# A seventh zero fill that leaves out one transfer engine

## The chip, the cores and the metric

The kernel runs on one core of a Trainium2 chip. The core has five engines that run their own instruction streams: TensorE (PE: matrix products, transposes), VectorE (DVE), ScalarE (ACT), GpSimd (POOL) and SyncE (SP). Data moves between the chip's main memory (HBM) and the on-chip memory through 16 transfer (DMA) engines. A transfer is issued by an engine's instruction stream; here nearly all are issued by POOL and some by SP. A transfer of 128 rows is cut into 16 shares of 8 rows, one for each transfer engine; each engine works through its shares in order, and raises the transfer's semaphore when its share is done.

The metric is the device time of one execution in microseconds (us). Before the change it is 599.19 us, the median of three runs (598.75 to 599.40).

## What is computed

The reference is a forward and a backward pass of one decoding step: one token of width 1024 through an adaptive layer norm with attention over the last 4096 positions of a key/value cache, and then through a gated feed-forward block. Cut to what matters:

```python
x = A_x
mod = (silu(c) @ w_mod).reshape(1, 6, 1, -1)
sa, ca, ga, sb, cb, gb = mod[:, 0], mod[:, 1], ..., mod[:, 5]
h = layernorm(x) * (1 + ca) + sa
x = x + ga * attention(h, k_cache[:, :, -4096:], v_cache[:, :, -4096:], wq, wo)
h = layernorm(x) * (1 + cb) + sb
x = x + gb * ((sigmoid(h @ w_gate) * (h @ w_up)) @ w_down)
out, grads = x, vjp(grad_out)   # gradients of x, caches, wq, wo, w_gate, w_up, w_down, c, w_mod
```

All tensors are bfloat16. The caches are [1, 4, 65536, 128]. Only the last 4096 positions of each head are used, so the gradients of both caches are zero in the first 61440 positions of each of the four heads: 2 x 4 x 61440 x 128 values, 120 MiB of zeros to be written.

## The kernel before

Everything that is loaded or computed lives in one large on-chip tile (`arena`) and some small ones. The weights are read once; their gradients, outer products of a column and a broadcast row, are made in place by VectorE and ScalarE, and stored. In order of time the kernel does the following. It loads w_mod, the key cache, wq and the value cache, and computes the query, the scores and the softmax. From about 70 us to 155 us it forms a product of keys and values (`n_ps`, L640), then from about 155 to 310 us a long product with w_o (`b_ps`, L695). The feed-forward block's loads, products, outer products and stores run in seven rounds (L1023 to L1068) until about 477 us. The last stage stores the gradients of w_o (`dwo`, L1142, in rows of 8 KB), of w_mod (`sec`, L1136, and `s2`, L1190), of wq (`dwq_tile`, L1186) and of the caches' last 4096 positions (`grad_kv`, L1167). The last ten stores go through SyncE's queue (`tail`, L1307 to L1314), the others through POOL's.

The order of the instructions is written out by hand. The zeros are written by 120 fills of 1 MiB each, and the calls `zero(n)` put them between the other transfers of POOL's queue, as many at each place as tables such as `Z_N`, `Z_B`, `Z_FFN` and `Z_END` say. A fill takes one of 120 regions, 128 rows of 8 KB, from the list `zleft`, and writes it from a small tile of zeros. `zero_rest`, called once after the query's products (L479), is issued at 54.5 us.

A fill is either wide or narrow. The list `NARROW` gives the places in the order of issue, counted from 0, at which a fill is narrow. A wide fill writes all 128 rows, 8 rows on each of the 16 transfer engines. A narrow fill is made of three instructions: POOL's cursor for the choice of transfer engines is reset (L160), a small transfer of `NS` = `SKIP` + 1 = 5 rows is issued (L162), which is meant for the engines 0 to 4, and then rows 8 to 127 of the region are written as 60 rows of two pieces (L165), which are meant for the 15 engines from 5 on, around to 3. By the code's plan engine 4 has no share of the narrow fill, and the others have the same share as in a wide one. The first 8 rows of the narrow regions, 64 KB each, are left over. They form `rest`, a block of 8 rows. Most of it is written by `zero_rest` with one transfer over 16 rows of pieces (L362) and a small one (L365); the pieces that are still missing are the small transfers of L162.

`keep`, `nlen` and `ncount` follow from the length of `NARROW`. The last stage's fills stand at these places:

```python
Z_END = (1, 2, 1, 0, 0)
zero(Z_END[0])          # L1194, before the stores of dwo(0) to dwo(3)
zero(Z_END[1])          # L1218, after dwo(5): two fills
zero(Z_END[2])          # L1244, after dwo(7): the last fill
```

Of the kernel before, what the change touches and what calls it, by code (L numbers as in the profile page):

```python
# [34 lines left out]
SCALE = DH ** -0.5  # L35
KIB = 512
SKIP = 4
NARROW = (15, 45, 75, 95, 104, 113)


def spread(total, n):
# [17 lines left out]
def kernel(  # L59
# [70 lines left out]

    narrow = zregions[0:len(NARROW)]
    wide = zregions[len(NARROW):]
    zleft = []
    while narrow or wide:
        if narrow and (len(zleft) in NARROW or not wide):
            zleft.append((narrow.pop(0), True))
        else:
            zleft.append((wide.pop(0), False))
    nlen = len(NARROW)
    ncount = list(range(1, nlen + 1))  # L140
# [1206 lines left out]
```

## Time and profile before

| what | value |
|---|---|
| median of three runs | 599.19 us (598.75 to 599.40) |
| the profiled execution: its time, its span | 599.24 us, 597.5 us |
| busy: PE, DVE, ACT, POOL | 68%, 56%, 44%, 26% of the span |
| moved by the transfer engines | 246.63 MB, 413 GB/s in the mean |
| HBM read, written | 60.30 MB, 185.60 MB |
| POOL's queue (q0), SP's queue (q1): share of 16 engines | 95.1%, 13.0% |
| wide fills | 114, 1024 KB each, 15.4 us from issue to landing |
| narrow fills | 6, 960 KB each, 12.8 us |
| the small transfers of narrow fills | 6, 2.5 KB each, 11.2 us |
| `zero_rest` | 360 KB, 10.7 us, and 9 KB, 10.4 us |
| the chain that ended last | PE 44%, DMA 22%, DVE 20% |

The span runs from the first to the last instruction of the profiled execution; the execution's own time is 1.7 us longer. Busy time of an engine says how much it worked, not what the kernel waited for. The page's slices cut the span into 40 equal parts, and their digits are tenths of a part. The shares of the two queues add up to more than 100%, since packets of both queues are under way on an engine at once. The page's chain of work follows the last instruction back to what released it, step by step. A transfer's time to landing runs from its issue to the moment at which all 16 transfer engines have done their share; most of it is the wait behind the transfers that were issued earlier.

### The profile page before, as it was taken

The numbers are of one execution on the slowest core, as the hardware profiler recorded it, in microseconds if no ns is written. First come the engines' busy times: TensorE is split into PE (matmuls) and PEld (weight loads), VectorE is DVE, ScalarE is ACT, GpSimd is POOL, SyncE is SP. The second block draws the span as 40 slices with busy tenths as digits, with TensorE's granted clock in tenths as the row PEclk, the third lists the DMA queues.
The fourth block names the chain that finished last, engine by engine and source line by source line (L and its number), as shares of the span: only waits on it lengthen the run. The fifth ranks groups of instructions, "written<-read, shape, count | busy, mean of one in ns | idle before, by whom it ended". The sixth has DMA issues, their size and how long they took to land.

```text
span 597.5 us, 11109 instructions
## 1 busy us (share of the span) xinstructions
PE 407.2 (68%) x4618; PEld 275.0 (46%) x4644; DVE 335.4 (56%) x642; ACT 264.9 (44%) x409; POOL 155.9 (26%) x254
## 2 busy tenths in 40 slices
PE   3997688999999989999983437245345285685210
PEld 3995334334344545546653326245334264485110
DVE  3654499999511010070018585678787886878350
ACT  2489514567211014212135275465664834893110
POOL 3113123222222213222221242323424252132100
PEclk9999699999999999999995565665555586955555
DMA  8999999999999999999999999999999999999996
GB/s 349 417 418 423 411 427 409 429 422 426 428 417 425 423 427 424 422 423 423 424 396 414 419 411 416 410 369 416 408 406 412 419 420 424 423 422 426 425 424 286
DMA packets 44003, 246.63 MB, mean 413 GB/s; under 512 B 5086, under 2 KB 5086, under 8 KB 22497
## 3 DMA queue, kind: packets, MB, share of 16 engines
q0 software_dynamic: 36656, 218.64, 95.1%
q1 hardware_dynamic: 7248, 27.27, 13.0%
q8 instruction: 36, 0.59, 0.4%
q14 instruction: 15, 0.11, 0.0%
q10 hardware_dynamic: 48, 0.01, 0.0%
HBM read 60.30 MB, written 185.60 MB: 412 GB/s over the span
## 4 chain that ended last, share of the span: by engine, by line
PE 44%; DMA 22%; DVE 20%; issue 5%; ACT 5%; POOL 0%; DVEq 0%; ACTq 0%; POOLq 0%; SPq 0%
PE b_ps L695 18%; DMA out_dram<-arena 14%; DVE arena L210 7%; PE n_ps L640 6%; DVE arena L206 5%; DMA arena<-in_B_w_down_dram 4%; DVE arena L193 4%; DMA arena<-in_B_w_gate_dram 3%; PE t_ps L602 2%; PE fold_ps L879 2%; PE tp_wq L457 2%; PE w_ps L398 2%; PE tp_side L840 1%; PE tp_k L438 1%; ACT arena L459 1%
## 5 line engine op out<-in xcount | busy, mean ns | idle before, releaser
L695 PE MATMUL b_ps<-arena 128*128 128x512 bf16 x493 | 113.4, 379 | 1.1 <-issue 0.2
L169 POOL DMA_DIRECT2D out_dram<-zeros x114 | 62.4, 549 | 175.1 <-DMA out_dram<-zeros 46.1
L193 DVE TENSOR_TENSOR arena<-arena 128x2048 bf16<-128x2048 bf16 x64 | 76.5, 1223 | 2.3 <-PE n_ps L640 0.3
L695 PEld LDWEIGHTS <-arena 128*128 128x128 bf16 x512 | 48.8, 98 | 55.8 <-issue 2.9
L210 DVE CUSTOM_DVE_ANT_0 arena<-arena,scr 128x1024 bf16<-128x1024 bf16 x56 | 66.3, 1221 | 9.7 <-ACT scr L995 9.7
L640 PE MATMUL n_ps<-arena 128*128 128x512 bf16 x249 | 65.1, 378 | 6.9 <-DVE arena L193 5.0
L841 ACT COPY arena<-tp_side 128x1024 bf16<-128x1024 bf16 x54 | 52.9, 1015 | 37.4 <-PE tp_side L840 37.4
L957 PE MATMUL fg<-h_bf,arena 128*128 128x1 bf16 x448 | 16.1, 166 | 52.0 <-DMA arena<-in_B_w_up_dram 31.4
L840 PE MATMUL tp_side<-ident_bf,arena 128*128 128x128 bf16 x432 | 47.9, 292 | 3.9 <-ACT arena L841 2.1
L840 PEld LDWEIGHTS <-arena 128*128 128x128 bf16 x432 | 41.5, 137 | 6.4 <-issue 6.1
L640 PEld LDWEIGHTS <-arena 128*128 128x128 bf16 x256 | 24.6, 97 | 41.6 <-issue 16.2
L241 ACT ACTIVATE arena<-scr,h 128x1024 bf16<-128x1024 bf16 x35 | 38.5, 1142 | 2.7 <-DVE dh2acc L210 2.3
L957 PEld LDWEIGHTS <-arena 128*128 128x128 bf16 x448 | 14.1, 105 | 55.0 <-DMA arena<-in_B_w_up_dram 33.1
L202 DVE CAST arena<-b_ps 128x512 bf16<-128x512 f32 x6 | 4.2, 692 | 61.6 <-PE b_ps L695 61.6
L210 DVE CUSTOM_DVE_ANT_0 arena<-arena,b1k 128x1024 bf16<-128x1024 bf16 x24 | 28.4, 1220 | 18.1 <-PE fg L975 18.1
L1176 ACT ACTIVATE arena<-ps_kv 128x512 bf16<-128x512 f32 x48 | 26.1, 681 | 27.2 <-PE ps_kv L1172 27.0
L1172 PE MATMUL ps_kv<-junk,arena 8*128 8x128 bf16 x256 | 26.6, 300 | 14.5 <-DVE arena L206 12.7
L872 POOL DMA_DIRECT2D out_dram<-arena x28 | 22.2, 798 | 50.9 <-ACT arena L241 36.2
L604 ACT CAST arena<-t_ps 128x512 bf16<-128x512 f32 x56 | 30.1, 589 | 12.1 <-PE t_ps L602 12.1
L1172 PEld LDWEIGHTS <-arena 8*128 8x128 bf16 x256 | 24.7, 138 | 16.2 <-issue 16.2
L459 ACT COPY arena<-tp_wq 128x1024 bf16<-128x1024 bf16 x23 | 21.7, 1042 | 8.2 <-PE tp_wq L457 8.2
L206 DVE TENSOR_SCALAR arena<-arena,cs_col 128x4096 bf16<-128x4096 bf16 (+1 forms) x16 | 16.2, 1031 | 10.4 <-DMA out_dram<-arena 10.3
(308 smaller groups left out, 637.8 us busy)
## 6 DMA issues: line engine op xcount, KB each, us to landing
out_dram<-zeros POOLq DMA_DIRECT2D x114, 1024.0 KB, 15.4
out_dram<-arena POOLq DMA_DIRECT2D x28, 1024.0 KB, 18.7
out_dram<-arena POOLq DMA_DIRECT2D x30, 512.0 KB, 12.0
out_dram<-arena SPq DMA_DIRECT2D x20, 512.0 KB, 9.3
arena<-in_A_wq_dram POOLq DMA_DIRECT2D x8, 1024.0 KB, 20.3
arena<-in_A_wo_dram POOLq DMA_DIRECT2D x8, 1024.0 KB, 11.9
arena<-in_w_mod_dram POOLq DMA_DIRECT2D x7, 1024.0 KB, 18.0
arena<-in_B_w_down_dram SPq DMA_DIRECT2D x14, 512.0 KB, 9.0
```

Source lines behind the costliest of these rows:

```text
L169: ins = nc.gpsimd.dma_start(out=region.bitcast(FP32), in_=zeros[:, :])
L193: return nc.vector.tensor_tensor(out=out, in0=a, in1=b, op=op)
L206: return nc.vector.tensor_scalar(out=out, in0=a, scalar1=s1, scalar2=None, op0=op0)
L210: return nc.vector.tensor_tensor_reduce(out=out, in0=w, in1=b, scale=1.0, scalar=0.0, op0=ALU.mult, op1=ALU.add, accum_out=acc)
L241: return nc.scalar.activation(out=out, in_=b, func=ACT.Copy, scale=col)
L604: nc.scalar.copy(out=o, in_=ps)
L640: mm = nc.tensor.matmul(nbank[k][:, :], lhsT=k_nat[:, g, t_ * DH:(t_ + 1) * DH], rhs=vp[:, t_ % 2, 4 * k:4 * k + 4, :].rearrange("p h d -> ...
L695: mm = nc.tensor.matmul(bbank[p][k][:, :], lhsT=a4[:, p, h, :], rhs=wo_t[u][:, a, k * 512:(k + 1) * 512], start=(i == 0 and a == 0), stop= ...
L840: nc.tensor.transpose(tp[:, i * P:(i + 1) * P], blk[:, i * P:(i + 1) * P], ident_bf[:, :])
L841: nc.scalar.copy(out=blk if dst is None else dst, in_=tp[:, :])
L957: nc.tensor.matmul(gu[:, col:col + 1], lhsT=ug_v[:, q % 2, j // 4, j % 4, k, f0:f0 + 255:2], rhs=h2_bf[:, j:j + 1], start=(j == 0 and i == ...
L1172: nc.tensor.matmul(ps[:, t4 * DH:(t4 + 1) * DH], lhsT=rows[32 * g:32 * g + HG, t_ * P:(t_ + 1) * P], rhs=hd[32 * g:32 * g + HG, :], start= ...
```

## The change

One number is added to `NARROW`:

```diff
-NARROW = (15, 45, 75, 95, 104, 113)
+NARROW = (15, 45, 75, 95, 104, 113, 117)
```

The fill at place 117 of 0 to 119 becomes narrow: the third from last, which is the first of the two fills at L1218. At that place POOL now issues the cursor's reset, the small transfer of 5 rows and the narrow fill of 120 rows, in place of a wide fill. `nlen` goes from 6 to 7, so `rest` grows from 6 x 64 KB to 7 x 64 KB, and the transfers of `zero_rest` grow with it: the pieces of L362 from 720 to 840 elements of 4 bytes, those of L365 from 768 to 896. Region 6 of the list becomes narrow too, and the wide fills take the regions after it, so that each writes the region that the next one wrote before. The number of 1-MiB places, their places in POOL's queue, and all instructions of the other engines stay as they are.

## The prediction

> **What bounds the kernel now.** I read the page's slices of the transfer engines first, then the transfers at the very end, then the chain that ended last, then the issues around the changed fill.
>
> ```profile
> DMA  8999999999999999999999999999999999999996
> GB/s 349 417 418 423 411 427 409 429 422 426 428 417 425 423 427 424 422 423 423 424 396 414 419 411 416 410 369 416 408 406 412 419 420 424 423 422 426 425 424 286
> ```
>
> The 16 transfer engines are busy in every slice, mostly at 410 to 427 GB/s; only the last slice falls far, to 6 tenths and 286 GB/s. So the kernel is as long as its transfers, and what is left to win lies where not all 16 work. The end in finer windows (DMA share is the last column but one):
>
> ```profile
> 585.00:590.00 5.00, 0.00 (x0) 0.00 (x0) 0.00 (x0) 0.00 (x0) 0.00 (x0) 0.50 1.01 421
> 590.00:591.00 1.00, 0.00 (x0) 0.00 (x0) 0.00 (x0) 0.00 (x0) 0.00 (x0) 0.50 0.99 406
> 591.00:592.00 1.00, 0.00 (x0) 0.00 (x0) 0.00 (x0) 0.00 (x0) 0.00 (x0) 0.50 0.84 344
> 592.00:593.00 1.00, 0.00 (x0) 0.00 (x0) 0.00 (x0) 0.00 (x0) 0.00 (x0) 0.50 0.53 217
> 593.00:594.00 1.00, 0.00 (x0) 0.00 (x0) 0.00 (x0) 0.00 (x0) 0.00 (x0) 0.50 0.21 86
> 594.00:595.00 1.00, 0.00 (x0) 0.00 (x0) 0.00 (x0) 0.00 (x0) 0.00 (x0) 0.50 0.06 25
> 595.00:596.00 1.00, 0.00 (x0) 0.00 (x0) 0.00 (x0) 0.00 (x0) 0.00 (x0) 0.50 0.07 29
> ```
>
> A share of 0.06 is one engine of 16, at 25 to 29 GB/s. From 594 to 596 us one engine works alone. The trace's completion records say it exactly: every transfer over all engines raises its semaphore 16 times, once for each engine. For the last store (issued at 576.94) the 16 arrivals are, in us:
>
> ```
> 591.31 591.39 592.08 592.13 592.68 592.73 592.83 592.90
> 592.90 592.96 592.97 593.73 594.04 594.19 594.24 596.54
> ```
>
> One engine is 2.30 us behind the next. The chain and SyncE say that nothing but transfers is left there:
>
> ```profile
> 543.94 21.55 DMA out_dram<-arena
> ...
> 565.51 5.05 DVE arena L206 x8
> ...
> 571.78 4.31 DVE arena L206 x6
> ```
>
> ```profile
> 574.79 0.72 SPq L1188 DMA_DIRECT2D out_dram<-arena  x1
> 575.60 2.53 SPq L1192 DMA_DIRECT2D out_dram<-arena  x2
> ```
>
> VectorE's last work ends at 576.1 us and the last store is issued at 576.94, some 19.6 us before it has landed. The end is the backlog of the latest engine and no engine's arithmetic.
>
> **Is the late engine the one that a narrow fill leaves out?** The trace does not number the engines, but the arrivals identify it. Around the narrow fill issued at 178 us, the arrivals relative to their median run: one of them creeps, +0.40, +0.47, +0.59, +0.62 over four transfers; after the narrow fill that one is gone, a new earliest one stands at -1.76, and it creeps again, -1.61, -1.49, while the other 15 keep their places. The one left out thus moved by 0.62 + 1.76 = 2.38 us. Around the narrow fill at 98 us one moves from +0.41 to -1.91, 2.32 us, and then creeps by about 0.1 us per fill (-1.91, -1.79, -1.70, -1.60). So the engine left out is the one that loses about 0.1 us in each fill. Before the last narrow fill (issued at 478) the latest arrival creeps the same way, +1.03, +1.25, +1.38, +1.53; after it nothing is later than +0.81. From 513 us on the latest arrival creeps once more: +0.94, +1.09, then with two steps back to +1.53, +1.93, +2.12, and up to +3.42 at 556. Creep and place agree: the late engine of the end is the one left out. That is a reading of order and drift, not a numbered record, and a rival below doubts it.
>
> **The change part by part.**
>
> *The seventh narrow fill.* It replaces the first of the two wide fills at L1218, issued at 493.81. A narrow fill leaves 64 KB of its region out, the share of one engine; the two moves above price it at 2.32 and 2.38 us for that engine; I take 2.35. For the other 15 the pair (small transfer plus narrow fill) took 2.47, 2.44, 2.23 and 2.39 us on the median arrival at the four narrow fills with no SyncE traffic beside them, against 2.44 for a wide fill: between -0.21 and +0.03; I take 0.
>
> *More small remainder.* The rest transfers at L362 and L365 grow by 7/6. L362 moved the median arrival from 63.51 to 64.45, 0.94 us, on all engines; a sixth more is 0.16 us for each of them. Ends: 0 (it lands early, and time between could absorb it, though no slice shows room) and 0.3 (double, as its rows get another odd length). I take 0.16.
>
> *POOL's issue.* One more instruction (0.61 us) and a longer one (0.67 for 0.53) at 493.8, with a cursor reset that takes no visible time:
>
> ```profile
> 477.92 0.61 POOL L162 DMA_DIRECT2D out_dram<-zeros  x1
> 478.51 0.67 POOL L165 DMA_DIRECT2D out_dram<-zeros  x1
> 479.17 0.59 POOL L169 DMA_DIRECT2D out_dram<-zeros  x1
> ...
> 493.28 0.53 POOL L1145 DMA_DIRECT2D out_dram<-arena  x1 [0.97 <-DVE arena L206]
> 493.81 0.54 POOL L169 DMA_DIRECT2D out_dram<-zeros  x1
> 496.17 0.53 POOL L169 DMA_DIRECT2D out_dram<-zeros  x1 [1.82 <-DMA out_dram<-zeros]
> 500.60 0.53 POOL L1145 DMA_DIRECT2D out_dram<-arena  x1 [3.90 <-DVE arena L206]
> ...
> 507.88 0.53 POOL L1145 DMA_DIRECT2D out_dram<-arena  x1 [0.57 <-DVE arena L206]
> 508.45 0.53 POOL L169 DMA_DIRECT2D out_dram<-zeros  x1
> ```
>
> The wait at 496.17 ended when the transfer eight places earlier (issued 481.56) had landed at 495.88: POOL keeps eight transfers under way. The small one takes one place of the eight, so the fill now at 496.17 would wait for a landing at 498.45, and the one at 508.45 for 511.03, each about 2.5 us later. Behind the first stands dwo(6) (500.60, it waits for VectorE anyhow), behind the second sec(2), issued at 511.58. The cover is the queue: the shortest time on POOL's queue in this stage from issue to the first arrival is 12.3 us (531.95 to 544.28). So nothing is priced; without that cover the two waits would cost up to 5.0 us. SyncE's queue is not passed.
>
> *Who waits for the late engine meanwhile.* The landing at 565.49 that releases VectorE is its arrival; the next stands at 563.47. VectorE and the ten last stores may start up to 2.0 us earlier. They join a backlog, so this is worth 0.
>
> **Sum.** Late engine: 596.54 - 2.35 + 0.16 = 594.35. Next engine: 594.24 + 0.16 = 594.40. The end moves from 596.54 to 594.40, by 2.14 us. Three others (594.04, 594.19, 594.24) stand within 0.2 us there, and the latest of several that scatter is a little later than each; I add 0.1. The profiled execution took 599.24 (span 597.5 and 1.7 around it), against a median of 599.19, so both are the same within their spread (598.75 to 599.4): 599.2 - 2.0 = 597.2 us.
>
> **Two rules weighed against these rows.** The small transfer landed 0.17 to 0.21 us after its forerunner and the pair was no longer than a wide fill. The Trainium skill (DMA: Bandwidth & Descriptors, Anatomy of one DMA) gives a transfer from this queue a fixed 2.0 us; by that as a cost in the queue the sum would be 2.14 - 2.0, a gain of 0.1, an estimate that the rows contradict. The arrivals show one creeping engine, the one left out. The same page (Latency and other measured facts) calls engines 7 and 15 the usually slow ones; by that, leaving out 4 helps an engine that isn't late and the sum is a loss of 0.16; no record here bears a number to test it by, the creep speaks against it.
>
> **Rivals.** (1) *Another engine takes the end.* An engine near the front is delayed by something that does not show in this order: the instruction load at 95.6 moved one arrival by 1.33 us (+0.31 to +1.64). With 0.7 to 1.3 us of it on one of the four engines at 594, the time is 597.9 to 598.5. For it: 36 such loads run; against it: none of TensorE's instructions is touched, so they should come where they came. (2) *The change does not do what it says*: the engine left out is not the one late at the end, for instance because the creeping one after 513 us is another. Then all engines get 0.16 us more: 599.4. Against it speaks the arrival that vanished after 478. (3) *Slower: POOL's eight places.* If the two later waits emptied the queues, the 5.0 us would outweigh the 2.1: 602.1. It decides once issues trail by more than the 12.3 us of cover; the profile shows 2.5.
>
> **How the numbers follow.** Forecast 597.2, chance 0.77, its own range 596.5 to 597.9 (gain 2.7 to 1.3: scatter of the latest arrivals and of the runs). Rival 1: 0.12, rival 2: 0.06, rival 3: 0.05. The range 596.5 to 598.8 takes in the first two and leaves out about 0.13. What this kernel's measurement can tell from no change is about 0.2%, 1.2 us, so 598.0 parts faster from same: faster 0.78 (forecast and the edge of rival 1), same 0.16, slower 0.06.
>
> **What would show it.** Right: the share of 0.06 at the end is gone or under 0.5 us; the last store's latest arrival is within 0.6 us of the second; the latest arrival just after 513 us falls from +0.94 to under +0.5 with a new earliest one near -1.5 or before. Wrong: one engine alone at the end as before (rival 2); waits of POOL over 3 us at L169 and falling DMA slices near 500 (rival 3); a different lone engine at the end (rival 1).

## The result, and the profile after

| | before | after |
|---|---|---|
| median of 22 runs each | 599.06 us | 597.62 us |
| lowest, highest | 597.99, 601.38 | 596.78, 599.81 |
| ratio of the times, 95% interval | | 0.998 [0.9971, 0.999] |
| profiled execution, span | 599.24, 597.5 | 599.12, 597.3 |

The change makes the kernel faster by 1.44 us by the medians, 0.24% of the time; the interval of the ratio makes that 0.6 to 1.7 us (0.001 and 0.0029 of 599.06). The forecast was 597.2 us, and 597.62 lies in its range. The profiled execution of after is one of its longer ones, 1.5 us above its median, and where it lost them is a finding of its own below. The page's slices of the transfer engines in after:

```profile
DMA  8999999999999999999999999999999999999998
GB/s 349 419 419 419 412 426 413 425 425 422 427 419 427 421 427 426 420 426 422 423 395 415 418 411 416 411 355 415 390 404 407 416 419 422 422 421 427 425 425 333
```

The last slice rose from 6 tenths and 286 GB/s to 8 tenths and 333. Slice 27 (from 388 us) fell from 369 to 355, slice 29 (from 418 us) from 408 to 390. Finer windows show the end of after. The columns are the stretch, its length, busy time of PE, PEld, DVE, ACT and POOL, TensorE's granted clock, the share of the transfer engines and their GB/s:

```profile
592.00:593.00 1.00, 0.00 (x0) 0.00 (x0) 0.00 (x0) 0.00 (x0) 0.00 (x0) 0.50 1.03 422
593.00:594.00 1.00, 0.00 (x0) 0.00 (x0) 0.00 (x0) 0.00 (x0) 0.00 (x0) 0.50 0.72 295
594.00:595.00 1.00, 0.00 (x0) 0.00 (x0) 0.00 (x0) 0.00 (x0) 0.00 (x0) 0.50 0.45 184
595.00:596.00 1.00, 0.00 (x0) 0.00 (x0) 0.00 (x0) 0.00 (x0) 0.00 (x0) 0.50 0.07 29
596.00:597.50 1.50, 0.00 (x0) 0.00 (x0) 0.00 (x0) 0.00 (x0) 0.00 (x0) 0.50 0.00 0
```

Before, the share was down at 0.53 by 592 to 593 us, and one engine went on alone for two more microseconds after 594. Here all engines work at full rate until 593, and then they end nearly together; one is alone for 0.77 us. The last store's arrivals (the 16 completion records of one transfer, one from each engine) say it to the hundredth; only the last five are shown:

```
before   593.73 594.04 594.19 594.24 596.54    the last is alone by 2.30
after    595.27 595.45 595.46 595.64 596.41    the last is alone by 0.77
```

POOL's issues around the changed place in after (start, length, line, transfer, and in brackets the wait before it and what ended that):

```profile
495.94 0.53 POOL L1145 DMA_DIRECT2D out_dram<-arena  x1 [0.96 <-DVE arena L206]
496.54 0.60 POOL L162 DMA_DIRECT2D out_dram<-zeros  x1
498.70 0.67 POOL L165 DMA_DIRECT2D out_dram<-zeros  x1 [1.56 <-DMA out_dram<-zeros]
501.15 0.58 POOL L169 DMA_DIRECT2D out_dram<-zeros  x1 [1.77 <-DMA out_dram<-arena]
503.91 0.56 POOL L1145 DMA_DIRECT2D out_dram<-arena  x1 [2.18 <-DMA out_dram<-arena]
...
513.34 0.53 POOL L169 DMA_DIRECT2D out_dram<-zeros  x1 [1.65 <-DMA out_dram<-zeros]
```

The small transfer (L162) and the narrow fill (L165) stand where one wide fill stood. The next fill comes 2.45 us after the narrow one's issue instead of 2.36 after the wide one's, the waits are 1.6 to 2.2 us, and no later slice of the transfer engines falls. The chain at the end is of the same kind as before:

```profile
545.27 20.35 DMA out_dram<-arena
565.65 5.67 DVE arena L206 x8
...
571.91 4.31 DVE arena L206 x6
```

VectorE's last work is about as far from the end as it was, and the last store is issued at 577.07, 19.3 us before it has landed.

### The profile page after: what moved, and what is told of

It reads as the page before. It is cut to its first block, busy times and chain, and to the rows that moved or that the text cites. A ratio compares the mean times of both kernels' runs of the same rounds, so it can differ in the third digit from the quotient of the medians.

```text
span 597.3 us, 11110 instructions
## 1 busy us (share of the span) xinstructions
PE 411.9 (69%) x4618; PEld 279.1 (47%) x4644; DVE 335.9 (56%) x642; ACT 265.0 (44%) x409; POOL 157.0 (26%) x255
## 4 chain that ended last, share of the span: by engine, by line
PE 44%; DMA 24%; DVE 17%; issue 6%; ACT 5%; POOL 1%; ACTq 0%; DVEq 0%; POOLq 0%; SPq 0%
PE b_ps L695 18%; DMA out_dram<-arena 15%; DMA arena<-in_B_w_gate_dram 6%; PE n_ps L640 6%; DVE arena L210 5%; DVE arena L206 5%; DVE arena L193 4%; PE t_ps L602 2%; DMA arena<-in_B_w_down_dram 2%; PE fold_ps L879 2%; PE tp_side L840 2%; PE w_ps L398 2%; PE tp_wq L457 2%; ACT arena L841 1%; PE tp_k L438 1%
## 5 line engine op out<-in xcount | busy, mean ns | idle before, releaser
L872 POOL DMA_DIRECT2D out_dram<-arena x28 | 22.3, 799 | 50.4 <-ACT arena L241 35.3
L868 POOL DMA_DIRECT2D arena<-in_B_w_up_dram x14 | 10.7, 765 | 45.5 <-PE tp_side L840 15.1
```

## The experiments

Each group of experiments ran on a chip of its own, beside the kernel before (598.98, 598.99 and 599.01 us in the three groups); each ratio is to that.

**First group: which engine, and does the place matter?** The first theory took over the prediction's view with a sharper edge: engine 4 is short of time over the whole kernel, so what counts is how much it is spared in all, wherever that happens. The rivals: the engine relieved is a neighbour, or the last narrow fill helps for another reason than its engine.

*The changed kernel once more* (no edit).

> The changed kernel once more, for a second profiled execution. Its first one took 599.12 us, 1.5 us above its median of 597.62, and its arrivals fell 1.5 us behind those of before between 395 and 457 us, ahead of the changed fill. Load theory (the end is set by the transfer engine with the most to do, and engine 4 has lost 2.4 us of it): about 1.4 to 2.0 us under the kernel before, 597.0 to 597.7; in an execution near the median the last store's latest arrival stands at 594.4 to 595.0 and the arrivals at 480 us are 0.16 us behind those of before. Rival (the change itself brings the loss of 1.5 us in the feed-forward rounds): every execution shows arrivals at 480 us 1.5 us or more behind, and those times that look fast are fast for another reason.

Measured: 598.10 us (597.39 to 598.40), ratio 0.9985 [0.9975, 0.9995]. Its end in windows:

```profile
592.00:593.00 1.00, 0.00 (x0) 0.00 (x0) 0.00 (x0) 0.00 (x0) 0.00 (x0) 0.50 0.70 287
593.00:594.00 1.00, 0.00 (x0) 0.00 (x0) 0.00 (x0) 0.00 (x0) 0.00 (x0) 0.50 0.36 147
594.00:595.00 1.00, 0.00 (x0) 0.00 (x0) 0.00 (x0) 0.00 (x0) 0.00 (x0) 0.50 0.19 78
595.00:596.00 1.00, 0.00 (x0) 0.00 (x0) 0.00 (x0) 0.00 (x0) 0.00 (x0) 0.50 0.00 0
```

The lone engine is gone; the last arrival, 595.41, is 0.25 us behind the next. The end is 1 us earlier than in the first profile of the changed kernel, so that one's extra time belonged to the execution. The time is over the 597.0 to 597.7 that the first theory gave, and the mean arrival of the rounds' last store was 0.55 us behind that of before, where 0.16 was expected.

*Engine 2 in place of engine 4.* The seventh narrow fill's small transfer has 3 rows and not 5, so that the 15 engines of the narrow fill begin at engine 3 and leave out engine 2; what the small transfer no longer writes goes into a third remainder transfer of 1 KB after `zero_rest`.

```diff
+    SKIPS = [4, 4, 4, 4, 4, 4, 2]
-                    out=rest[0:NS, 0:nlen * 128].rearrange("p (t x) -> p t x", t=2)[:, :, n * 64:(n + 1) * 64],
-                    in_=zeros[0:NS, 0:64].rearrange("p (t x) -> p t x", t=1).broadcast_to([NS, 2, 64]))
+                    out=rest[0:SKIPS[n] + 1, 0:nlen * 128].rearrange("p (t x) -> p t x", t=2)[:, :, n * 64:(n + 1) * 64],
+                    in_=zeros[0:SKIPS[n] + 1, 0:64].rearrange("p (t x) -> p t x", t=1).broadcast_to([SKIPS[n] + 1, 2, 64]))
...
+        for n, k in enumerate(SKIPS):
+            if k + 1 < NS:
+                nc.gpsimd.dma_start(
+                    out=rest[k + 1:NS, 0:nlen * 128].rearrange("p (t x) -> p t x", t=2)[:, :, n * 64:(n + 1) * 64],
+                    in_=zeros[0:NS - k - 1, 0:64].rearrange("p (t x) -> p t x", t=1).broadcast_to([NS - k - 1, 2, 64]))
```

> The seventh narrow fill leaves out engine 2 in place of engine 4; all else as in the changed kernel, but for one more transfer of 1 KB at the start. Load theory: engine 4 keeps its load, stands alone at the end again by about 2 us (DMA share 0.06 from 594 to 596), and the time is that of before plus 0.2: 599.2. Rival (any shorter fill at that place, the moved regions or the other issue order bring the gain): as the changed kernel, 597.6. Rival (the late engine is not the one that the code calls 4, but its neighbour): also a gain.

Measured: 599.43 us (598.14 to 601.00), ratio 1.0005 [0.9991, 1.0018]. No gain. Its last arrival, at 598.31, is 1.21 us behind the next (this profiled execution took 601.0):

```profile
594.00:595.00 1.00, 0.00 (x0) 0.00 (x0) 0.00 (x0) 0.00 (x0) 0.00 (x0) 0.50 0.26 107
595.00:596.00 1.00, 0.00 (x0) 0.00 (x0) 0.00 (x0) 0.00 (x0) 0.00 (x0) 0.50 0.17 70
596.00:597.50 1.50, 0.00 (x0) 0.00 (x0) 0.00 (x0) 0.00 (x0) 0.00 (x0) 0.50 0.09 36
```

The arrivals around the fill, relative to their median, tell the two engines apart. In this kernel a new earliest one appears at -2.62, then -2.91, -2.89, -2.90: after its first step it does not creep back. In after the new earliest one is at -2.07, then -2.00, -1.90, -1.78: it loses about 0.1 us in each transfer. The engine that the code calls 4 is the one that loses time, and of the two that were tried only sparing that one helps.

*The seventh narrow fill at place 30 instead of 117.*

```diff
-NARROW = (15, 45, 75, 95, 104, 113, 117)
+NARROW = (15, 30, 45, 75, 95, 104, 113)
```

> The seventh narrow fill stands at place 30 (near 135 us) and not at 117 (near 494 us). Load theory: what counts is an engine's whole load, as none of them ever runs out of work, so the gain is the same, 597.3 to 597.8. Rival (the place counts: a lead won early is lost again, by creeping or by waits, before the end): 598.5 to 599.2, with the lone engine back at the end. POOL's window of eight transfers near 500 us is as before the change, so if those waits cost anything, this is faster than the changed kernel by it.

Measured: 599.48 us (598.05 to 599.65), ratio 1.0006 [0.9997, 1.0014]. No gain: the first theory falls. The same seven fills spare the same engine as often, and the time depends on where. The lone engine is back, at 596.40, 1.81 us behind the next.

*Both places, eight narrow fills.*

```diff
-NARROW = (15, 45, 75, 95, 104, 113, 117)
+NARROW = (15, 30, 45, 75, 95, 104, 113, 117)
```

> An eighth narrow fill at place 30 beside the seventh at 117, both leaving out engine 4. Load theory: engine 4 now ends 2 us before the others, which have 0.16 us more each: 0 to 0.3 us over the changed kernel, 597.6 to 597.9. Rival (every fill less on engine 4 is worth 1.4 us or more): 596.0 to 596.3.

Measured: 597.84 us (596.86 to 600.40), ratio 0.999 [0.9977, 1.0002]: no more than the changed kernel. The fill at place 30 brings nothing here either.

**Where does an early relief go?** The windows of the feed-forward rounds in before answer it:

```profile
385.00:390.00 5.00, 3.88 (x69) 3.72 (x70) 0.39 (x3) 2.12 (x4) 0.00 (x0) 0.50 1.25 420
390.00:395.00 5.00, 1.91 (x50) 1.73 (x48) 4.57 (x9) 2.99 (x4) 1.63 (x2) 0.84 1.02 366
395.00:400.00 5.00, 3.15 (x28) 2.74 (x28) 3.61 (x10) 2.35 (x3) 2.74 (x4) 0.50 0.99 356
400.00:405.00 5.00, 0.74 (x16) 0.58 (x16) 5.00 (x9) 4.93 (x6) 0.00 (x0) 0.50 1.08 401
405.00:410.00 5.00, 4.08 (x68) 3.65 (x68) 4.38 (x12) 3.46 (x6) 2.69 (x4) 0.50 1.15 406
```

From 390 to 400 us the transfer engines move 356 to 366 GB/s where 420 went before. POOL's issues show why:

```profile
390.44 0.75 POOL L868 DMA_DIRECT2D arena<-in_B_w_up_dram  x1 [5.49 <-PE fg L975]
393.02 0.88 POOL L868 DMA_DIRECT2D arena<-in_B_w_gate_dram  x1 [1.83 <-DMA out_dram<-arena]
396.37 0.88 POOL L868 DMA_DIRECT2D arena<-in_B_w_up_dram  x1 [2.47 <-issue]
...
405.22 1.71 POOL L872 DMA_DIRECT2D out_dram<-arena  x2 [5.71 <-ACT arena L241]
```

POOL waits for TensorE, then for a store to land, and between 399 and 405 for ScalarE. Meanwhile the queues of the engines that are ahead run dry, and those behind catch up. The arrivals relative to their median (first three, last three of 16) show the levelling:

```
             median     earliest              latest
before       395.08     -2.79 -2.77 -2.63     +1.13 +1.16 +2.02
before       401.84     -0.38 -0.33 -0.31     +0.48 +0.52 +1.63
place 30     394.68     -3.13 -2.95 -2.74     +1.26 +1.46 +2.68
place 30     402.14     -1.03 -0.78 -0.30     +0.85 +0.88 +2.19
```

In before, 15 engines that were spread over 3.9 us stand within 0.9 us seven microseconds later. What an engine had gained until then is gone. The narrow fills themselves let the engine left out be followed: at each of them one arrival leaves its place and moves forward by about 2 us, and that one is its own. Just before the fills issued at 356 and at 428 us it stood, relative to the median, at

```
             before 356 us   before 428 us
before       +0.79           +0.39
before again +0.74           +0.73
place 30     -1.08           +0.25
```

The lead of 1.9 us that place 30 gave it is there at 356 us; at 428 us what is left of it, 0.14, is less than two executions of the kernel before differ by (0.34). So a second theory: the balance between the engines counts only from the last place at which queues run dry, and a narrow fill ahead of about 395 to 450 us is worth nothing at the end.

**Second group: a place just ahead of the dry stretch, one just behind it, and an early fill taken out.**

*The kernel before once more* (no edit).

> The kernel before, unchanged, for a second profiled execution and as a measure of the scatter. Dry-queue theory: arrivals at 480 us scatter by up to 1.5 us between executions of any of these kernels, with the bytes not moved between 395 and 450 us; the lone engine stands at the end by about 2 us whatever the time. Rival (the changed kernel itself loses 0.6 to 1.5 us in that stretch, the kernel before does not): arrivals at 480 us as in the first execution, within 0.2 us. Ratio 1.000 within 0.1%.

Measured: 598.94 us (598.02 to 603.00), ratio 1.0002 [0.9984, 1.0021]. Its profiled execution took 598.19. The end in windows:

```profile
592.00:593.00 1.00, 0.00 (x0) 0.00 (x0) 0.00 (x0) 0.00 (x0) 0.00 (x0) 0.50 0.63 258
593.00:594.00 1.00, 0.00 (x0) 0.00 (x0) 0.00 (x0) 0.00 (x0) 0.00 (x0) 0.50 0.35 143
594.00:595.00 1.00, 0.00 (x0) 0.00 (x0) 0.00 (x0) 0.00 (x0) 0.00 (x0) 0.50 0.10 41
595.00:596.00 1.00, 0.00 (x0) 0.00 (x0) 0.00 (x0) 0.00 (x0) 0.00 (x0) 0.50 0.00 0
```

The last arrivals are 594.60, 594.71 and 595.51. One engine is alone here too, but by 0.80 us and not by 2.30, so the expectation of about 2 us "whatever the time" was wrong. This is the number that the prediction lacked.

*Place 98*, whose fill lands at 392 us in the median, just ahead of the dry stretch, *and place 108*, whose fill lands at about 470 us, behind it.

```diff
-NARROW = (15, 45, 75, 95, 104, 113, 117)
+NARROW = (15, 45, 75, 95, 98, 104, 113)
```

> The seventh narrow fill at place 98, issued near 380 us and landed near 390, just ahead of the stretch from 395 to 450 us in which the rates of the kernel before fall to 356, 401, 400 and 398 GB/s and the 16 arrivals draw together to 2 us. Dry-queue theory (a lead won before that stretch is lost there, since the engines ahead run out of work and wait for the same next issue): no gain, 599.0 to 599.6, as with place 30, and the lone engine back at the end. Rival (a lead fades bit by bit with time, so place 98 keeps most of it): 597.6 to 598.2.

```diff
-NARROW = (15, 45, 75, 95, 104, 113, 117)
+NARROW = (15, 45, 75, 95, 104, 108, 113)
```

> The seventh narrow fill at place 108, issued near 455 us and landed near 470, behind the last of the slow stretches (440 to 450 us, 398 GB/s). Dry-queue theory: the whole gain, 597.4 to 598.1, the latest arrival of the last store within 1 us of the next. Rival (only the place at the very end counts, since a lead fades with time): in the middle between before and the changed kernel or less, 598.2 to 599.0.

Measured on the same chip: place 98 took 599.67 us (598.87 to 601.61), ratio 1.0006 [0.999, 1.0022]; place 108 took 597.79 us (597.06 to 600.73), ratio 0.9978 [0.9963, 0.9993]. Ten places further on, the same fill is worth 1.9 us more. The end with place 98:

```profile
594.00:595.00 1.00, 0.00 (x0) 0.00 (x0) 0.00 (x0) 0.00 (x0) 0.00 (x0) 0.50 0.40 164
595.00:596.00 1.00, 0.00 (x0) 0.00 (x0) 0.00 (x0) 0.00 (x0) 0.00 (x0) 0.50 0.21 86
596.00:597.50 1.50, 0.00 (x0) 0.00 (x0) 0.00 (x0) 0.00 (x0) 0.00 (x0) 0.50 0.04 16
```

and with place 108:

```profile
593.00:594.00 1.00, 0.00 (x0) 0.00 (x0) 0.00 (x0) 0.00 (x0) 0.00 (x0) 0.50 0.34 139
594.00:595.00 1.00, 0.00 (x0) 0.00 (x0) 0.00 (x0) 0.00 (x0) 0.00 (x0) 0.50 0.13 53
595.00:596.00 1.00, 0.00 (x0) 0.00 (x0) 0.00 (x0) 0.00 (x0) 0.00 (x0) 0.50 0.00 0
```

With place 98 the last arrival is 1.24 us behind the next, with place 108 0.16. The arrivals show where the lead goes. With place 98 the engine left out is the earliest, at -3.56 and -3.55, in the two stores behind its fill (medians 393.22 and 394.50); in the loads that follow, the earliest of all 16 arrivals is at -1.64, -0.49 and -0.40 (medians 395.89, 398.21 and 401.17), and in the next stores (412.88) at -0.51. So the lead is lost within some seven microseconds, and not bit by bit. With place 108 the engine keeps its lead: it is the earliest, at -2.14, before the fill issued at 479 us, where it was at +1.53 in before, and that fill moves it on to -4.23. The second theory holds.

*Place 15 taken out, place 117 kept*: six narrow fills again, as before the change, one of them moved.

```diff
-NARROW = (15, 45, 75, 95, 104, 113, 117)
+NARROW = (45, 75, 95, 104, 113, 117)
```

> The changed kernel without its narrow fill at place 15: six in all, the seventh at 117 kept, so the small remainder is that of before. Engine 4 carries 2.4 us more from 105 us on. Dry-queue theory: as long as it does not become the engine on whose landings the stages wait, that load is levelled in the slow stretch and costs nothing, and the smaller remainder gives 0.16 us back: 597.3 to 598.0. Rival (the whole sum over the execution counts): the end is again engine 4's, 599.0 to 599.4. Rival (a late engine 4 delays the loads between 105 and 395 us, and with them the feed-forward rounds): over 599.5.

Measured: 597.84 us (596.78 to 599.84), ratio 0.9974 [0.996, 0.9988], the same as the changed kernel. The last two arrivals are 594.21 and 594.22:

```profile
593.00:594.00 1.00, 0.00 (x0) 0.00 (x0) 0.00 (x0) 0.00 (x0) 0.00 (x0) 0.50 0.21 86
594.00:595.00 1.00, 0.00 (x0) 0.00 (x0) 0.00 (x0) 0.00 (x0) 0.00 (x0) 0.50 0.00 0
```

So the gain is not that of a seventh narrow fill; it is that of one more behind the dry stretch. The engine left out lags by as much as it was spared less, and loses that lag in the same place: it stands at +2.72 before the fill at 356 us (+0.79 in before), and at +0.99 before the one at 428.

**Third group: how far can that be carried, and can the dry stretch be filled?**

*Only the four late narrow fills.*

```diff
-NARROW = (15, 45, 75, 95, 104, 113, 117)
+NARROW = (95, 104, 113, 117)
```

> The changed kernel without its narrow fills at places 15, 45 and 75; 95, 104, 113 and 117 are kept. Engine 4 carries up to 7.1 us more than the others' share allows by 395 us, and the remainder is 4/7 of that of the changed kernel. Dry-queue theory with a bound: the stretch from 395 to 450 us can level only as much as an average engine stands idle there, 1.5 to 2.5 us; what is over it delays landings that the feed-forward rounds wait for, so slower than the changed kernel by 2 to 5 us: 599.6 to 603. Rival (any load ahead of that stretch is levelled, the early narrow fills do nothing): 597.0 to 597.8.

Measured: 601.33 us (599.98 to 602.35, and one execution of 694.97 that nothing here explains; 601.23 without it), ratio 1.0028 [1.0011, 1.0045]. Slower, by 0.7 to 2.7 us. Without relief engine 4 falls far back before the rounds begin (it is the arrival that the first narrow fill, at 361 us, moves, from +5.06 to +3.01): the latest arrival is 5.97 us behind the median at 287 us and 8.66 at 299 us, where after has 2.41 and 3.11. The rounds' loads then wait for it: the 16 arrivals of the fourth load of gate and up run from 307.04 to 317.15. One stretch of the rounds in this kernel, and the same in after:

```profile
345.00:360.00 15.00, 5.48 (x68) 4.84 (x68) 11.50 (x25) 11.05 (x11) 4.83 (x7) 0.61 0.95 323
```

```profile
345.00:360.00 15.00, 3.98 (x56) 3.24 (x54) 12.04 (x24) 9.79 (x10) 7.21 (x10) 0.61 1.11 411
```

From 345 to 360 us it moves 323 GB/s where after moves 411: the queues run dry here too, by 88 x 15 us, 1.3 MB or 3.1 us at 425 GB/s. The loads of the later rounds are issued some 6 us later than in after (355.43 for 349.52). An early narrow fill is thus worth nothing at the end, but enough of them must keep the late engine from holding up what waits for all 16.

*One more fill into the dry stretch*, taken from the end of the kernel: in the third round, and in another kernel in the fourth. The narrow places move by one where needed, so that the late ones stay at their transfers.

```diff
-NARROW = (15, 45, 75, 95, 104, 113, 117)
+NARROW = (15, 45, 75, 95, 105, 114, 118)
-Z_FFN = [(1, 1, 0, 2), (1, 1, 0, 1)] + [(1, 0, 0, 2)] * 3 + [(1, 1, 1, 2), (1, 2, 1, 0)]
-Z_END = (1, 2, 1, 0, 0)
+Z_FFN = [(1, 1, 0, 2), (1, 1, 0, 1)] + [(1, 1, 0, 2), (1, 0, 0, 2), (1, 0, 0, 2)] + [(1, 1, 1, 2), (1, 2, 1, 0)]
+Z_END = (1, 2, 0, 0, 0)
```

> The changed kernel with one wide fill moved from behind dwo(7) in the last stage to a place ahead of the loads of the third feed-forward round (near 385 us), where the queues run dry afterwards; the narrow fills keep their neighbours. Dry-queue theory, if the idle time there can take a fill: the last stage is 2.4 us shorter and the stretch 395 to 405 us moves more bytes, up to 1.5 us under the changed kernel: 596.1 to 597.6. Rival (those loads are what the round waits for, so that a fill ahead of them delays the round by its 2.4 us and only moves the gap): as the changed kernel or up to 1 us over it, 597.6 to 598.6.

The other kernel has `[(1, 0, 0, 2), (1, 1, 0, 2), (1, 0, 0, 2)]` in the middle.

> As the run before, with the fill one round later, ahead of the loads of the fourth round (near 410 us); the stretch that it should fill is 420 to 430 us, where 378 to 402 GB/s were moved. Dry-queue theory: up to 1 us under the changed kernel, 596.6 to 597.6. Rival (the loads are late by the fill's 2.4 us and the gap moves on): 597.6 to 598.6.

Measured: 598.16 us (597.02 to 599.68), ratio 0.9985 [0.9969, 1.0], and 598.01 us (597.07 to 599.38), ratio 0.9983 [0.9969, 0.9998]. Neither is better than the changed kernel. The windows of the first:

```profile
395.00:400.00 5.00, 2.90 (x24) 2.47 (x24) 3.61 (x10) 2.33 (x3) 2.61 (x4) 0.50 1.06 394
400.00:405.00 5.00, 0.27 (x4) 0.18 (x4) 5.00 (x9) 4.93 (x6) 0.00 (x0) 0.50 1.04 389
...
420.00:430.00 10.00, 2.90 (x35) 2.31 (x33) 8.61 (x16) 8.25 (x8) 4.27 (x6) 0.50 0.98 355
```

The hole at 395 to 400 is filled, 394 GB/s for before's 356, and another opens at 420 to 430, 355 for 400. The second moves 335 GB/s at 395 to 400 and 397 at 420 to 430. That fits rounds that are paced by what waits for TensorE, VectorE and ScalarE there, so that a fill only moves the hole; no run takes those waits away, so it stays a reading. No kernel of this study is clearly faster than the changed one.

**All of them side by side.** The end part of a profiled execution runs from the mean arrival of the rounds' last store (L872, the 28th; at 485 to 489 us) to the last arrival of all. In the two kernels with a moved fill it holds other work, so they are left out:

| kernel | time, us | ratio | end part, us | last arrival alone by, us |
|---|---|---|---|---|
| before | 599.06 | | 111.12 | 2.30 |
| before, again | 598.94 | 1.0002 | 109.78 | 0.80 |
| place 30 | 599.48 | 1.0006 | 110.88 | 1.81 |
| place 98 | 599.67 | 1.0006 | 110.49 | 1.24 |
| engine 2 at 117 | 599.43 | 1.0005 | 111.57 | 1.21 |
| after (117) | 597.62 | 0.998 | 109.32 | 0.77 |
| after, again | 598.10 | 0.9985 | 109.44 | 0.25 |
| 30 and 117 | 597.84 | 0.999 | 109.40 | 0.72 |
| 108 | 597.79 | 0.9978 | 109.22 | 0.16 |
| 117 without 15 | 597.84 | 0.9974 | 108.75 | 0.01 |
| 95, 104, 113, 117 alone | 601.33 | 1.0028 | 108.63 | 0.10 |

Those without one more relief of engine 4 behind the rounds take 109.78 to 111.57 us for the end part, those with it 108.63 to 109.44. The means are 110.77 and 109.13, a difference of 1.6 us, near the 1.44 us of the times. Each row is one profiled execution, and the two groups come as near to each other as 0.34 us.

## Why the prediction was right, and where it was not

*The end is the backlog of one late engine, and that engine is the one left out.* Right. Engine 4 spared late gives 0.9974 to 0.9985 in four runs of kernels and 0.999 in a fifth; engine 2 spared at the same place gives 1.0005. With it rival 2 (the change does not do what it says) is out. The Trainium skill (DMA: Bandwidth & Descriptors, Latency and other measured facts) calls engines 7 and 15 the usually slow ones. No run here tests that: none left out 7 or 15, and no record says which number the engine that the code calls 4 has there.

*Another engine takes the end (rival 1).* In part: in after's own profile some engine is last by 0.77 us, and no record says which. Its forecast of 597.9 to 598.5 holds the 598.10 of the changed kernel's second series, the forecast of 597.2 is nearer the 597.62 of the first. No engine was set back far enough to take the place of the lone one.

*The size.* This is the term that was mis-sized: "Late engine: 596.54 - 2.35 + 0.16 = 594.35. Next engine: 594.24 + 0.16 = 594.40. The end moves from 596.54 to 594.40, by 2.14 us." The relief of 2.35 was near (in the second profile of the changed kernel the engine left out moved from about +0.7 to -1.39 and then -1.44, 2.1 us), but the 2.30 us by which the late engine ends behind the next are those of one execution. In the second profiled execution of the same kernel it was 0.80 us; the same sum there gives 595.51 - (594.71 + 0.16) = 0.64. The measured gain, 1.44, lies between 0.64 and 2.14. That the forecast came within 0.42 us of the measured time is thus in part luck: from the other profile the same working gives about 598.6, outside the forecast's own range of 596.5 to 597.9. The execution's own time was the median's, and that hid that its end was unusual: its rounds were short (the last store's mean arrival at 485.42, the earliest of all profiled executions) and its lone engine late. The engine left out stood at +1.53 before the fill at 478 us in that execution, and at about 0.0 in the second one; that difference is as large as that between 2.30 and 0.80, which fits but is shown by two executions only. The 0.1 us taken off for the scatter of several engines was meant for this, and too small.

*The remainder's 0.16 us.* Right: L362 moves the median arrival by 1.08 us in after (63.43 to 64.51) and 0.94 in before, 0.14 more, and with four narrow fills by 0.62 (63.53 to 64.15).

*The pair costs the other 15 engines nothing.* Right: the small transfer landed 0.20 us behind its forerunner in the median (511.61 to 511.81), the narrow fill 2.29 after it, 2.49 for the pair against 2.44 for a wide fill. The fixed 2.0 us of a transfer that the Trainium skill gives (DMA: Bandwidth & Descriptors, Anatomy of one DMA) is again not to be seen in the queue.

*POOL's eight places.* Right, and rival 3 false: the fill after the narrow one is issued at 501.15 (496.17 before), the last at 513.34 (508.45). That is 5.0 and 4.9 us later, 1.7 of it being this execution's lateness; in the second profile of the changed kernel, 0.55 us late, it is 3.6 and 3.5. So the change makes up some 3 us of it, where 2.5 was forecast. No wait of POOL between the narrow fill and the last one is over 2.54 us, and nothing behind it fell: 421 to 427 GB/s in the slices from 493 to 582 us.

*What the profile would show.* The lone engine was to be gone or alone for under 0.5 us, and the latest arrival within 0.6 us of the next: met in one of the two profiles of the changed kernel (0.25), just missed in the other (0.77). A new earliest arrival near -1.5 came, at -2.07 and -1.39. But the latest one did not fall from +0.94 to under +0.5: it was at +1.43 both before and after the new fill, and at +0.99 in the second profile. The arrivals that keep their places across the fill leave a gap between 0.0 and +0.3 in the first profile and at about +0.7 in the second: there the engine left out stood, inside the field and not at its end. "From 513 us on the latest arrival creeps once more" was a fair reading of one execution; that engine 4 is the last at 513 us was not a property of the kernel.

*What the prediction did not see.* "The 16 transfer engines are busy in every slice, mostly at 410 to 427 GB/s" passed over slice 27 with its 369 GB/s. It is the stretch in which the rounds run the queues dry and the engines are levelled. For this change nothing came of it, as place 117 lies behind it; for a change at place 30 or 98 the same working would have promised 2 us and got none. The same stretch holds the 1.5 us by which after's profiled execution is long. The mean of the 16 arrivals differs between before and after by 0.13 us at 372 us (the eighth store of the rounds) and by 1.67 at the rounds' last store, and the windows between show less moved:

```profile
395.00:400.00 5.00, 2.82 (x24) 2.58 (x25) 3.75 (x9) 1.93 (x2) 2.66 (x4) 0.50 1.02 324
400.00:405.00 5.00, 1.07 (x21) 0.74 (x19) 5.00 (x12) 4.61 (x5) 0.00 (x0) 0.50 1.01 371
...
420.00:430.00 10.00, 1.90 (x28) 1.39 (x26) 9.93 (x18) 7.06 (x7) 5.68 (x8) 0.50 1.04 378
```

These are after's 324, 371 and 378 GB/s where before has 356, 401 and 400: 32 x 5, 30 x 5 and 22 x 10 make 530 KB, 1.25 us at 425 GB/s. All of it lies ahead of the changed fill. The second profile of the changed kernel lost 0.55 us by 487 us, and the second of the kernel before 0.31. Six of the 22 first runs of the changed kernel took over 599.1 us, none of its 11 later ones did, so whether the change makes such executions more frequent stays open; by its mechanism nothing but the 0.16 us of the remainder, and the exchanged regions of the wide fills, reaches that stretch.

## What to carry to other kernels

Where transfers are the bound, look not only for the engine that ends last but for the last place at which queues run dry: balance between transfer engines that is won ahead of it is levelled away, and the same fill is worth nothing or 1.4 us by its place. Take the size of a tail from two or three executions; here one showed a lone engine by 2.30 us and the next by 0.80. A late engine still has to be kept near the others where arithmetic waits for whole transfers, as four late fills alone were about 2 us slower than before.

## What the runs showed of the hardware

- One of the 16 transfer engines is slower than the others: behind the narrow fills at 98 and 178 us in before, and behind the one at 499 us in after, it lost 0.07 to 0.15 us in each 1-MiB transfer of 2.44 us, while engine 2, spared in its place, kept its lead (-2.91, -2.89, -2.90). Without early relief the latest arrival was 8.66 us behind the median at 299 us. Why it is slower is not shown. Sparing it late, with at least three of the early fills kept, helped in all three groups of runs.
- A queue that runs dry for a few microseconds levels the engines: 15 of them went from a spread of 3.9 us to 0.9 us between 395 and 402 us in before, and the one that place 98 had put 3.55 us ahead of the median was no further ahead than 0.49 two loads later.
- How much the rounds lose in that stretch differs from execution to execution with the same instructions: the last store's mean arrival stood at 485.42 and 485.73 us in two of the kernel before, at 487.09 and 485.97 in two of the changed one.
